# One table of order, slots and engines for another: linear attention and a three-way feed-forward layer on one core

## The chip, the cores and the metric

The kernel runs on one core of one Trainium2 chip. The metric is the device time of that core in microseconds, as the median of several runs. The core has five engines with queues of their own: TensorE (PE, matrix products), VectorE (DVE), ScalarE (ACT), GpSimd (POOL) and SyncE (SP, which here only issues DMAs). POOL and ACT issue DMAs as well.

## The reference

Inputs and output are float32. The kernel computes in bfloat16, with the sums of products in float32.

```python
# q, k, v: (8 batches, 8 heads, 576 tokens, 64); w_phi: (64, 128)
def phi(x):
    proj = x @ w_phi
    proj = proj - max(abs(proj), axis=-1)
    return concatenate([exp(proj), exp(-proj)], axis=-1)
q_p, k_p = phi(q), phi(k)
kv = k_p.T @ v;  z = sum(k_p over tokens)
attn = (q_p @ kv) / (q_p . z + 1e-6)
x = attn as (4608 tokens, 512)
h = max(max(x @ w1, x @ w2), x @ w3)        # d_ff = 768
out = h @ w_out
```

The attention has no softmax over the tokens, so that all of a head's keys go into one matrix kv before its queries use it.

## The kernel before

**Attention.** The work is cut into 16 units. Unit u holds four heads of batch u // 2. For each unit the kernel loads q and k by POOL's DMA queue, which turns them into bf16 on the way (qk_bf, L432 and L442); the 64 last tokens of each head, the "tail", and v come by SP (tail_raw L475, v_raw L484). Then q and k are turned. In units 0 to 3 TensorE does that (tps, L508); from unit 4 on it is a DMA transposition issued by SP (qkT<-qk_bf, L527; 128x10x128 for the keys with the tails, 128x8x128 for the queries). TensorE projects by w_phi (L545, products of 64 rows), VectorE takes the largest absolute values (mk and mq, L549), ScalarE the exponentials of the keys (Ek, L553) and of the queries (Eq, L633). The factor of the keys' largest value goes into the values: POOL multiplies v by em (vab, L597). Then come the key-value products (kvps, L616, 64 rows), a second projection (psm, L642 and L650), the numerators with the denominator beside them (psn, L683), their sums on VectorE (y, L692 and L695), the reciprocal (rden, L740), and the division on POOL (x_sb, L741). The quotient is turned again, from unit 2 on by a DMA transposition on SP (xT<-x_sb, L773).

**Feed-forward layer.** Nine chunks: one of 512 tokens for each batch, and a ninth of all the tails (8 x 64 tokens). The weights come by POOL's queue; the kernel holds w2 - w1 and w3 - w1 (L987), so that the maximum over three becomes a relu of one difference (L905, L907) and a maximum with the other (L901), while the part through w1 goes straight through w1 times w_out (pm, L1023). A chunk then has up products (ups, L891), the straight products (L924), the down products (ops, L929), the evictions (osb<-ops, L939, on ScalarE or VectorE, into one of four buffers) and the stores (L943, on SP's queue but for one). The seventh, eighth and ninth chunk are computed with seven up products in the place of eight (L820): this needs four sums of quarters of xT for each chunk (sums, L799, on VectorE or POOL), joins on VectorE (parts and hT, L829), relu on ScalarE (L862) and a maximum on VectorE (hx in the code, hT<-hT,parts at L864).

**Order.** Everything is recorded first as a list of 1688 steps, each with the steps that it depends on and the buffers that it uses. Nothing is scheduled when the kernel is built: PLAN, a table of words written out in the program, gives for each step its engine, the slots of its buffers and its place. A word such as

```python
19T0@4.8      # step 19, TensorE, slot 0, start at 4.8
```

names the step, the engine (T, D, A, G, S for PE, DVE, ACT, POOL, SP), the slots and a planned start. plan() reads it and returns the steps in the order in which they are issued; each engine then runs its own steps in that order and waits by semaphores for what it depends on. The planned start has one more use: fill() puts products on a constant tile (idler, L1071) into the planned gaps of TensorE in the first 30 us.

Of the kernel before, what the change touches and what calls it, by code (L numbers as in the profile page):

```python
# [90 lines left out]
1D@0.8 4A@1.1 103G0@1.2 10S0@0.7 3S@1.1 9G1@1.9 8G@2.6 2D@0.9 16S0@1.7 11A@3.9 12D@3.9 7D@4.1 5D@4.3 102G@3.4 0G@4.1 19T0@4.8 20D0@5.2  # L91
6A@4.2 29T12@5.7 31A0@6.2 30A0@6.6 35D0@6.2 186G2@4.6 17G@8.4 104G@8.6 259G3@8.8 260G@9.6 106T3@7.3 107D1@8.0 13S@3.1 112T45@8.7
34A@7.1 33A@7.6 119T67@8.9 32D@8.6 114A1@9.1 185G@10.3 187S1@3.5 118D1@9.2 121A@9.6 113A1@10.1 110T0@9.2 25T3@9.4 111D@9.8 125D@9.9
122D@10.6 26D@11.2 15D@11.5 117A@10.6 23T2@11.4 18S1@4.9 123A@11.1 116A@11.5 120A@12.0 24A@12.5 124A@13.0 1166G@11.0 188G@11.8
1169G@12.0 51T10@11.8 115D@11.7 52D0@12.3 27T3@12.1 28D@12.9 14D@13.1 73T56@12.6 53D@13.3 74A0@13.4 105S2@5.6 1167G@12.7 75A0@13.9
76A@14.4 77A@14.9 21T2@13.5 22D@13.9 43T74@13.8 48T13@13.9 46D@14.3 49D@14.6 47D@15.2 50D@15.5 54A0@15.3 68T05@14.6 36T62@15.5
126T14@15.7 70A@15.6 44A@16.0 45A@16.3 69A@16.6 71A@17.0 72A@17.5 129D@16.1 42D@16.5 41A@18.0 333G1@13.9 334S0@9.0 108T3@16.3
130D1@17.1 39D@17.4 109D@18.0 78T7@16.8 190T0@17.2 1168G@15.2 141A1@18.5 80A@18.7 191D2@18.6 134T54@18.8 55G0@16.0 56G@17.1 403G0@18.5
261G@19.2 57G@19.4 265T3@19.1 58A@18.9 40A@19.1 131T02@19.8 135D@19.2 136D@19.8 266D3@20.4 62T54@20.5 144G1@19.6 59G@19.7 61G@20.8
60G@20.9 128A@19.6 79A@19.9 37A@20.1 127A@20.6 38A@20.9 137A@21.4 64A0@21.6 133D@21.0 132D@21.6 63D@22.2 151T37@21.1 263T1@21.5  # L100
153A1@21.7 152A1@22.2 81A0@22.7 194T6@21.9 195D@22.4 264D@22.6 65T42@22.2 67D@23.2 66D@23.4 155A@22.9 154A@23.3 85T05@22.8 82T36@23.1
161T1@23.5 86D0@23.6 192T2@23.6 162A@23.8 163A@24.1 83D@24.0 87D@24.4 193A@24.4 84D@24.8 90T47@24.0 156T01@24.5 91D1@25.2 93T35@25.0
402G@22.0 140G@22.8 139G@22.9 138G@24.0 142G@25.1 157A@25.2 94D@25.6 145T26@25.4 164A1@25.7 92D@26.0 95D@26.4 1188T4@26.1 160A@25.9
146A1@26.4 147A@26.6 1192T3@26.5 1189D0@26.8 165T75@27.0 158A@26.7 168T26@27.3 88D0@27.4 166D2@27.5 169D@27.9 404G@26.2 143G@26.4
332G@27.5 89G0@28.2 335G@29.4 1193A@27.2 159A@28.1 167D@28.3 96D1@28.7 170D@28.8 171D2@29.4 148T40@27.7 97G@29.7 1190T7@28.4 150A@28.6
149A@28.7 301T23@28.9 1191A@29.0 173T15@29.2 176T60@29.6 172G1@30.9 337S0@35.1 189S3@36.5 174D0@29.8 177D@30.2 175D@30.6 98T4@29.9
1198T7@30.1 178D@31.0 99D@31.4 753S0@42.1 303A0@29.9 302A0@30.4 305A@30.9 304A@31.4 262S1@42.8 406S1@43.5 179D0@31.8 276T16@31.5
196T50@31.8 267T4@32.1 1200T2@32.2 612S1@47.0 277A0@32.0 280A@32.4 1199D@31.9 281A0@32.9 180G@32.1 202D0@32.5 268D@33.1 279D1@33.3
100T3@33.5 183T7@33.8 1170G@33.6 1172G@35.7 101D@34.0 184D@34.4 282D@34.8 199D@35.4 1196T4@34.0 181T3@35.3 200A1@33.4 201A1@33.9
1201A@34.4 278A@34.8 1197A@35.5 182D@36.0 203T76@35.7 215T02@35.9 291T14@36.2 206D@36.4 1194T3@36.5 208A@36.1 197A@36.6 198A@37.1  # L110
205A@37.6 1195A@38.1 293D0@37.0 217D1@37.6 292D@38.2 204A@38.5 1214T5@38.0 216D@38.8 269T34@38.9 283T21@39.2 287D@39.5 1171G@37.8
1212T7@39.4 210T01@40.3 1215A1@39.0 207A@39.5 284A@40.0 275D@39.8 1173G@39.9 1175G@42.0 285A@40.3 271A@40.5 214D@40.7 213D@41.0
1213D@41.3 1206T5@40.5 274A@41.0 212A@41.5 211A@41.8 1207A@42.0 270A@42.5 273A@43.0 1204T1@41.4 1210T7@42.3 1211A@43.5 286D@41.9
336S2@48.6 209D@42.2 221A0@43.9 1205D@42.8 272D@43.4 1208T0@43.1 306T54@44.1 1209D@44.2 218T72@44.3 308A@44.5 307A@45.0 228T61@44.5
219D@44.8 407S@49.3 220D@45.4 1226T3@44.9 288T05@45.8 1174G@44.1 1218T7@46.1 289D@46.2 1227D@46.9 1224T2@47.0 224G0@46.2 1219D@47.5
290D@48.0 1225D@48.6 222G@46.5 229A1@45.5 294A1@46.0 309A@46.1 231A@46.6 310A@47.1 241A0@47.6 232A1@47.8 230A@48.3 233T03@48.0
236A@48.7 237A@49.2 223G@48.5 1216T7@48.3 238T5@49.1 339T24@49.4 1217D@49.4 353T16@49.6 225T37@50.5 342D0@50.0 356D@50.6 357D1@50.9
# [985 lines left out]
```

## Time and profile before

| | |
|---|---|
| time, three runs | 280.34, 281.12, 281.60 us; median 281.12 |
| profiled execution | 280.52 us, of which the span is 278.7 |
| granted TensorE clock | 0.999 of full speed, mean |
| PE busy | 269.0 us, 97% of the span |
| weight load of PE (overlaps) | 161.7 us, 58% |
| DVE | 243.5 us, 87% |
| ACT | 212.9 us, 76% |
| POOL | 186.7 us, 67% |
| DMA | 44.54 MB, mean 160 GB/s |

The profile shows one execution. Its span runs from the first instruction to the last; 1.8 us of the measured time lie outside. A line of the profile names the line of the program, the engine and the tiles (output<-inputs). The chain of waits is followed back from the last instruction: at each step to what released it, or to the instruction before it on its engine. A group in the page gives the busy time, the mean length of one and the idle time of the engine just before, with what ended it.

### The profile page before, as it was taken

The page shows a single profiled execution, that of the slowest core. Times are in us where ns is not written, and L with a number is a line of the kernel's source. Part 1 is how long each engine was busy: PE and PEld are TensorE (multiplying, and loading weights), DVE is VectorE, ACT ScalarE, POOL GpSimd, SP SyncE. Part 2 cuts the span into 40 slices and gives each one's busy share as a digit, 9 for nine tenths or more (in the row PEclk, how much of TensorE's full clock was granted, in tenths as well). Part 3 has the DMA queues.
Part 4 walks back from the last instruction along what each step waited for, and adds up shares of the span by engine and source line. Part 5 has one row for each costly group of instructions (what it writes and reads, how often), then busy time and mean ns, then how long its engine had stood idle before and what let it go on. Part 6 is the DMA issues. An engine that isn't in the chain of part 4 may idle for free.

```text
span 278.7 us, 8796 instructions
## 1 busy us (share of the span) xinstructions
PE 269.0 (97%) x3561; PEld 161.7 (58%) x3561; DVE 243.5 (87%) x497; ACT 212.9 (76%) x507; POOL 186.7 (67%) x184
## 2 busy tenths in 40 slices
PE   7989999999999989999999999999999998999993
PEld 5657654566555645555655456555548765686651
DVE  3899999999999869879889998999889999999950
ACT  3899999998899979598977999698988523254241
POOL 6789999998679634896397795888798844500000
PEclk9999999999999999999999999999999999999999
DMA  7999999999999999989999994940421242003434
GB/s 125 262 232 209 209 196 309 221 200 255 178 215 231 195 200 189 175 224 206 201 188 196 276 132 121 187 137 2 123 46 43 78 94 78 0 1 115 109 71 161
DMA packets 76216, 44.54 MB, mean 160 GB/s; under 512 B 52688, under 2 KB 67344, under 8 KB 76176
## 3 DMA queue, kind: packets, MB, share of 16 engines
q1 hardware_dynamic: 61184, 32.19, 53.6%
q0 software_dynamic: 14912, 11.77, 28.7%
q8 instruction: 28, 0.46, 0.7%
q14 instruction: 12, 0.10, 0.1%
q10 hardware_dynamic: 80, 0.03, 0.0%
HBM read 34.64 MB, written 9.44 MB: 158 GB/s over the span
## 4 chain that ended last, share of the span: by engine, by line
PE 83%; DVE 6%; ACT 4%; DMA 3%; issue 2%; POOL 1%; DVEq 0%; ACTq 0%; POOLq 0%
PE ups L891 23%; PE ops L929 15%; PE ops L924 10%; PE ups L820 7%; PE psn L683 7%; PE kvps L616 6%; PE psk L545 3%; PE psm L642 3%; DMA qkT<-qk_bf 3%; PE psq L545 3%; PE pm L1023 2%; ACT Ek L553 2%; DVE parts L829 2%; PE tps L508 1%; DVE hT L864 1%
## 5 line engine op out<-in xcount | busy, mean ns | idle before, releaser
L633 ACT ACTIVATE Eq<-psm 128x512 bf16<-128x512 f32 (+1 forms) x160 | 80.3, 583 | 6.8 <-PE psm L642 4.8
L553 ACT ACTIVATE Ek<-psk 128x512 bf16<-128x512 f32 x128 | 72.5, 639 | 5.8 <-PE psk L545 5.3
L597 POOL TENSOR_TENSOR vab<-v_raw,em 128x1152 bf16<-128x1152 f32 (+1 forms) x36 | 68.2, 1908 | 10.9 <-ACT em L591 10.9
L891 PE MATMUL ups<-xT,w_bf 128*128 128x512 bf16 x288 | 70.1, 379 | 0.0
L741 POOL TENSOR_TENSOR x_sb<-y,rden 128x640 bf16<-128x640 f32 x32 | 39.9, 1256 | 25.2 <-DVE rden L740 20.3
L929 PE MATMUL ops<-wout_bf,hT 128*128 128x512 bf16 (+2 forms) x222 | 52.1, 373 | 0.8 <-DVE hT L864 0.8
L549 DVE TENSOR_REDUCE mq<-psq 128x4 f32<-128x512 f32 x64 | 40.9, 681 | 4.0 <-PE psq L545 3.6
L549 DVE TENSOR_REDUCE mk<-psk 128x4 f32<-128x512 f32 x64 | 42.3, 681 | 1.7 <-PE psk L545 1.5
L891 PEld LDWEIGHTS <-w_bf 128*128 128x128 bf16 x288 | 25.0, 98 | 26.8 <-issue 1.7
L692 DVE TENSOR_TENSOR y<-psn,sq 128x325 f32<-128x325 f32 x64 | 30.3, 489 | 7.0 <-PE psn L683 6.2
L929 PEld LDWEIGHTS <-hT 128*128 128x128 bf16 x222 | 20.5, 98 | 22.1 <-DVE hT L864 1.3
L683 PEld LDWEIGHTS <-Eq 128*128 128x128 bf16 x640 | 26.5, 98 | 11.2 <-issue 0.9
L939 ACT COPY osb<-ops 128x512 f32<-128x512 f32 x28 | 16.8, 599 | 20.5 <-PE ops L929 19.6
L695 DVE TENSOR_TENSOR y<-y,psn 128x325 f32<-128x325 f32 x64 | 29.6, 484 | 1.5
L829 DVE TENSOR_TENSOR parts<-ups,parts 128x512 f32<-128x512 f32 (+1 forms) x45 | 29.1, 679 | 0.5
L683 PE MATMUL psn<-kv_sb,Eq 128*128 128x65 bf16 x640 | 28.9, 194 | 0.1
L545 PEld LDWEIGHTS <-qkT 64*128 64x128 bf16 x576 | 18.2, 94 | 15.4 <-issue 10.8
L901 DVE TENSOR_TENSOR hT<-hT,ups 128x512 bf16<-128x512 bf16 x36 | 23.9, 681 | 1.4 <-PE ups L891 1.0
L862 ACT ACTIVATE hT<-hT 128x512 bf16<-128x512 bf16 x18 | 10.7, 625 | 18.5 <-DVE hT L829 18.5
L924 PE MATMUL ops<-xT 128*128 128x512 bf16 x96 | 24.7, 380 | 0.0
L616 PE MATMUL kvps<-vab,Ek 64*128 64x65 bf16 x1152 | 22.1, 191 | 0.6 <-issue 0.5
L616 PEld LDWEIGHTS <-Ek 64*128 64x128 bf16 x1152 | 20.1, 94 | 2.5 <-issue 0.6
(85 smaller groups left out, 395.3 us busy)
## 6 DMA issues: line engine op xcount, KB each, us to landing
v_raw<-in_v_dram SPq DMA_DIRECT2D x16, 576.0 KB, 5.4
out_dram<-osb SPq DMA_DIRECT2D x32, 256.0 KB, 2.8
qk_bf<-in_k_dram POOLq DMA_DIRECT2D x15, 288.0 KB, 8.5
qk_bf<-in_q_dram POOLq DMA_DIRECT2D x15, 256.0 KB, 7.6
w_bf<-in_moe_w_dram POOLq DMA_DIRECT2D x3, 768.0 KB, 19.5
tail_raw<-in_q_dram SPq DMA_DIRECT2D x16, 64.0 KB, 5.5
wout_bf<-in_moe_w_out_dram POOLq DMA_DIRECT2D x1, 768.0 KB, 16.6
out_dram<-osb SPq DMA_DIRECT2D x6, 128.0 KB, 2.4
```

Of the source, the lines that this page charges most:

```text
L545: nc.tensor.matmul(ps[s]()[:, i, :], lhsT=qkT()[r, n, :], rhs=wph[r, :], start=True, stop=True)
L549: return nd(kind, {"DVE": 0.598 if n == 4 else 0.331}, lambda: nc.vector.tensor_reduce(dst(m()), ps()[:, 0:n, :], AXX, ALU.max, apply_abso ...
L553: return nd("ek", {"ACT": 0.478 if n == 4 else 0.264}, lambda: nc.scalar.activation(dst(Ek[g]()), ps()[:, 0:n, :], EXP, scale=1.0 - 2.0 * ...
L597: made.append(chosen(n_, lambda n_, g=g, t0=t0, t1=t1: (nc.vector if n_.eng == "DVE" else nc.gpsimd).tensor_tensor(vab()[:, g, t0:t1, 0:D] ...
L616: nc.tensor.matmul(kvps[ab]()[:, pr, g, :], lhsT=Ek[g]()[r, t, :], rhs=vab()[r, g, t, :], start=(pr == prs[0] and g + j == 0), stop=(pr == ...
L633: return nd("eq", {"ACT": 0.478 if n == 4 else 0.264}, lambda: nc.scalar.activation(Eq[g]()[:, t0:t0 + n, :], ps()[:, 0:n, :], EXP, scale= ...
L683: nc.tensor.matmul(psn[g]()[:, i, :], lhsT=Eq[g]()[:, t, :], rhs=kv()[:, pr, ab, g, :], start=True, stop=True)
L741: divs[pr] = nd("x", {"POOL": 1.2}, lambda pr=pr, y=y, rden=rden: nc.gpsimd.tensor_tensor(x_sb()[:, pr].rearrange("p t a d -> p a t d"), y ...
L829: return ff("uj", {"DVE": 0.598}, lambda: nc.vector.tensor_tensor(runs(dst()) if dst not in own else dst(), runs(ps()), runs(src()), ALU.add),
L891: nc.tensor.matmul(ups()[:, o * n:(o + 1) * n], lhsT=w_bf[i + (not plain)][:, ct, jj * P:(jj + 1) * P], rhs=tokens_of(ct)[:, cols] if halv ...
L924: nc.tensor.matmul(ops_()[:, 0:hi - lo], lhsT=tile_of(ct, tt), rhs=line_w[c_i > MOVE][:, ct, lo:hi], start=(ct == 0), stop=False)
L929: nc.tensor.matmul(ops_()[:, 0:hi - lo], lhsT=hT()[:, j, tt * P:(tt + 1) * P], rhs=wout_bf[:, j, lo:hi], start=plain and j == 0, stop=(j = ...
```

## The change

Only PLAN is another. The steps, their products, the functions and the line numbers are those of before. The first line of the table, before and after:

```diff
 PLAN = """
-1D@0.8 4A@1.1 103G0@1.2 10S0@0.7 3S@1.1 9G1@1.9 8G@2.6 2D@0.9 16S0@1.7 11A@3.9 12D@3.9 7D@4.1 5D@4.3 102G@3.4 0G@4.1 19T0@4.8 20D0@5.2
...
+3A@0.7 1D@0.8 4A@1.3 6D@3.7 103G0@1.2 10S0@0.7 5D@3.9 11A1@4.0 7A@4.3 9G@1.9 8G@2.6 0G@3.4 2D@4.1 12D@4.2 19T0@4.6 20D0@5.1 29T12@5.6
...
 """
```

59 of the 1688 steps change their engine: 26 go from VectorE to ScalarE and 21 back, 4 from POOL to ScalarE and 3 back, 2 from VectorE to POOL and 2 back, and the load of w_phi goes from SP to ScalarE. TensorE has the same products in another order, and 51 of the fillers at L1071 where there were 63. The slots are dealt out anew throughout. Three places of the order follow, each before and after. The numbers in the names only tell tiles apart, and are dealt anew in each build.

The first place is SP's queue around the transposition of unit 8's keys (qkT<-qk_bf in ten blocks, 128x10x128). The two rows of x_sb are the quotients of units 4 and 5, in this order; the rows of eight blocks are queries, and L943 is a store. Before:

```order
L943 DMA out_0_dram<-osb_1903 128x512
L773 DMA_TRANSPOSE xT_75<-x_sb_2089 128x10x128
L943 DMA out_0_dram<-osb_1810 128x512
L527 DMA_TRANSPOSE qkT_2526<-qk_bf_2126 128x10x128
L773 DMA_TRANSPOSE xT_75<-x_sb_2335 128x10x128
L527 DMA_TRANSPOSE qkT_2592<-qk_bf_2124 128x8x128
```

After:

```order
L943 DMA out_0_dram<-osb_1901 128x512
L527 DMA_TRANSPOSE qkT_1930<-qk_bf_1504 128x8x128
L475 DMA tail_raw_2166<-in_q_dram 64x4x64 x2
L527 DMA_TRANSPOSE qkT_2206<-qk_bf_2050 128x10x128
L773 DMA_TRANSPOSE xT_75<-x_sb_2180 128x10x128
L484 DMA v_raw_2242<-in_v_dram 128x2x576
L475 DMA tail_raw_2351<-in_q_dram 64x4x64 x2
L773 DMA_TRANSPOSE xT_75<-x_sb_2280 128x10x128
```

The transposition of unit 8's keys stood behind the quotient of unit 4 and a store; now it stands ahead of that quotient, and the store is not between them.

The second place is VectorE at the last maxima of the seventh chunk (L864 on tiles of 2x256) and the first joins of the ninth (hT of 16x32). Before:

```order
L829 TENSOR_TENSOR parts_5219<-ups_5416,parts_5446 128x512
L829 TENSOR_TENSOR hT_5259<-ups_5455,parts_5446 128x2x256
L829 TENSOR_TENSOR hT_5259<-ups_5468,parts_5411 128x2x256
L829 TENSOR_TENSOR parts_5387<-ups_5402,parts_5411 128x512
L829 TENSOR_TENSOR hT_5532<-ups_5510,parts_5526 128x16x32
L799 TENSOR_TENSOR sums_5534<-xT_75 128x512
L864 TENSOR_TENSOR hT_5259<-hT_5259,parts_5387 128x2x256
L864 TENSOR_TENSOR hT_5259<-hT_5259,parts_5219 128x2x256
```

After:

```order
L829 TENSOR_TENSOR hT_5213<-ups_5436,parts_5415 128x2x256
L829 TENSOR_TENSOR hT_5213<-ups_5426,parts_5410 128x2x256
L829 TENSOR_TENSOR parts_5209<-ups_5386,parts_5415 128x512
L799 TENSOR_TENSOR sums_5468<-xT_75 128x512
L799 TENSOR_TENSOR sums_5468<-sums_5468,xT_75 128x512
L864 TENSOR_TENSOR hT_5213<-hT_5213,parts_5182 128x2x256
L864 TENSOR_TENSOR hT_5213<-hT_5213,parts_5209 128x2x256
L829 TENSOR_TENSOR hT_5523<-ups_5481,parts_5501 128x16x32
```

VectorE had one sum there, of the eighth chunk; now it has two, of the ninth chunk, ahead of the last pair of maxima. On POOL the same stretch is the end of its work. Before (sums_5491 are the ninth chunk's, sums_5534 the eighth's):

```order
L1056 COPY x_late_76<-xT_75 128x4x64
L799 TENSOR_TENSOR sums_5491<-xT_75 128x512
L799 TENSOR_TENSOR sums_5491<-sums_5491,xT_75 128x512
L799 TENSOR_TENSOR sums_5491<-xT_75 128x512
L799 TENSOR_TENSOR sums_5534<-sums_5534,xT_75 128x512
L799 TENSOR_TENSOR sums_5491<-xT_75,sums_5491 128x512
L799 TENSOR_TENSOR sums_5534<-xT_75 128x512
L799 TENSOR_TENSOR sums_5534<-xT_75,sums_5534 128x512
```

After (sums_5468 are the ninth chunk's, sums_5525 the eighth's):

```order
L1056 COPY x_late_76<-xT_75 128x4x64
L799 TENSOR_TENSOR sums_5468<-xT_75 128x512
L799 TENSOR_TENSOR sums_5468<-xT_75,sums_5468 128x512
L799 TENSOR_TENSOR sums_5525<-xT_75 128x512
L799 TENSOR_TENSOR sums_5525<-sums_5525,xT_75 128x512
L799 TENSOR_TENSOR sums_5525<-xT_75 128x512
L799 TENSOR_TENSOR sums_5525<-xT_75,sums_5525 128x512
```

The ninth chunk's second and third sums went from POOL to VectorE, and the eighth chunk's first from VectorE to POOL.

The third place is SP's queue from the keys of unit 4 to the values of unit 4. The three value loads before are those of units 2, 10 and 3, in this order. Before:

```order
L527 DMA_TRANSPOSE qkT_895<-qk_bf_408 128x10x128
L484 DMA v_raw_897<-in_v_dram 128x2x576
L484 DMA v_raw_918<-in_v_dram 128x2x576
L484 DMA v_raw_926<-in_v_dram 128x2x576
L527 DMA_TRANSPOSE qkT_928<-qk_bf_469 128x10x128
L475 DMA tail_raw_962<-in_q_dram 64x4x64 x2
L484 DMA v_raw_1135<-in_v_dram 128x2x576
L527 DMA_TRANSPOSE qkT_928<-qk_bf_469 128x8x128
```

After (the value loads are those of units 2, 3, 4 and 6):

```order
L527 DMA_TRANSPOSE qkT_624<-qk_bf_330 128x10x128
L484 DMA v_raw_836<-in_v_dram 128x2x576
L527 DMA_TRANSPOSE qkT_880<-qk_bf_575 128x10x128
L475 DMA tail_raw_948<-in_q_dram 64x4x64 x2
L484 DMA v_raw_1094<-in_v_dram 128x2x576
L484 DMA v_raw_1124<-in_v_dram 128x2x576
L484 DMA v_raw_1153<-in_v_dram 128x2x576
L527 DMA_TRANSPOSE qkT_624<-qk_bf_330 128x8x128
```

The values of unit 3 were issued right behind those of units 2 and 10, and now stand behind the keys of unit 5 and a tail load.

More of the change, by code (lines that the diff above doesn't have):

```diff
@@ L239 @@
[L239 removed]
+3A@0.7 1D@0.8 4A@1.3 6D@3.7 103G0@1.2 10S0@0.7 5D@3.9 11A1@4.0 7A@4.3 9G@1.9 8G@2.6 0G@3.4 2D@4.1 12D@4.2 19T0@4.6 20D0@5.1 29T12@5.6
+34A0@6.0 32D0@6.0 35D@6.7 106T3@7.4 102G@3.9 260G2@4.6 16S0@1.1 186G3@5.3 185G@6.1 259G@6.8 104G@8.1 31A@6.8 30A0@7.3 110T4@8.5
+111A1@8.8 33A@9.1 1166G@8.3 17G@9.1 107D@8.1 112T56@8.8 118D1@9.3 119T70@9.1 115D@9.9 13S@2.5 15D@10.5 25T1@10.0 1169G@10.0 14D@10.7
@@ new lines @@
+1404T6@193.0 1049A@193.9 1405A@194.1 1050A@194.6 1110T14@194.0 1117T07@194.2 1020D@193.9 1113D@194.4 1120D@195.0 1121D1@195.3
+1116D@195.7 957S@192.0 1416T5@194.4 1420T6@195.3 1021T32@196.1 1417D@196.3 1022D@196.9 1421D@197.3 1412T7@196.4 1418T5@197.3
+1061G0@192.4 1060G@194.5 1112A@195.2 1111A@195.7 1128A1@196.4 1118A@196.6 1119A@196.9 1115A@197.2 1114A@197.7 1145T3@198.2
+1010T61@198.3 1146A0@198.5 1023D@197.9 1419D@198.4 1011D@199.0 1024D1@199.4 1147A1@198.7 1413A@199.0 1131G1@196.8 1129G@196.9
@@ L240 @@
+1553D@263.7 1586T2@261.9 1587T@262.8 1588D0@264.3 1562D@264.9 1590T3@264.1 1583T@265.0 1589S@265.1 1674S@265.7 1584A1@266.5 1585S@267.1
+1543D@265.3 1595T@266.3 1596D2@267.8 1597S@268.5 1591T@267.6 1592A0@269.1 1593S@269.7
 """
```

288 lines of the change are left out of this document (140 added, 148 removed).

## The prediction

> **What bounds the kernel now.** I read the page first, then the busy time by stretch, the waits of TensorE, the chain of waits and single stretches of the timeline. On the page, the shares of the chain by engine:
>
> ```profile
> PE 83%; DVE 6%; ACT 4%; DMA 3%; issue 2%; POOL 1%; DVEq 0%; ACTq 0%; POOLq 0%
> ```
>
> TensorE carries 83% of the chain. A busy TensorE need not be at its peak, so I cut the span where its state changes (columns: stretch, length, then busy us of PE, PEld, DVE, ACT, POOL, granted clock, DMA share, GB/s):
>
> ```profile
> 0.00:27.00 27.00, 23.80 (x357) 16.83 (x359) 20.95 (x49) 21.84 (x56) 21.68 (x37) 1.00 1.11 207
> 27.00:92.00 65.00, 64.66 (x970) 37.61 (x970) 61.86 (x133) 62.23 (x150) 57.68 (x50) 1.00 1.19 223
> 92.00:101.00 9.00, 7.98 (x141) 4.46 (x140) 6.51 (x13) 7.31 (x21) 6.21 (x5) 1.00 1.28 189
> 101.00:211.00 110.00, 109.95 (x1588) 60.97 (x1587) 97.40 (x199) 94.76 (x231) 80.33 (x74) 1.00 0.88 162
> 211.00:232.50 21.50, 20.64 (x243) 14.67 (x236) 21.02 (x44) 9.89 (x23) 15.98 (x17) 1.00 0.22 56
> 232.50:267.00 34.50, 34.48 (x251) 23.88 (x250) 32.88 (x59) 13.77 (x25) 4.77 (x5) 1.00 0.20 63
> 274.60:278.70 4.10, 0.00 (x0) 0.00 (x0) 0.00 (x0) 0.59 (x1) 0.00 (x0) 0.94 0.17 65
> ```
>
> From 27 us on TensorE stops only in two places, for 1.0 us of 9.0 around 92 to 101 and for 0.9 us of 21.5 before 232.5, and the last 4.1 us are the last eviction and store. Before 27 us it is not the bound: part of its 23.8 us are the filler products of L1071. The waits of TensorE name both places (us in total, times, longest):
>
> ```profile
> PE psk L545 <- DMA qkT<-qk_bf: 1.0, 1, 1.0
> PE ops L929 <- DVE hT L864: 0.8, 1, 0.8
> ```
>
> The change leaves the products as they are, so it can win only in such waits, in what a product costs by its neighbours, and in the first 27 us.
>
> **1. Fewer changes between forms of product.** The chain shows what a change costs (start, us, what):
>
> ```profile
> 46.17 0.97 PE ups L891 x4
> 47.14 0.33 PE psq L545 x8
> ...
> 54.01 0.37 PE psn L683 x10
> 54.37 0.87 PE ups L891 x4
> ```
>
> Four up products take 0.97 us when the rows next to them are 64-row products (L545, L616, L642), and 0.87 when they follow full ones (L683): 0.10 us for a change. Counted over the whole printed order, leaving out the fillers and L650, which runs in either form, there are 114 such changes before and 102 now. From the first L924 on, where every TensorE microsecond counts, there are 73 before and 67 now. I take 6 x 0.10 = **-0.6 us**; the bounds are 0 and all 12, -1.2.
>
> **2. The keys of unit 8.** The wait of 1.0 us is for a transposition on SP's queue; SP's timeline, with the POOL operation that released the first of its rows, and the transposition in the chain:
>
> ```profile
> 90.02 1.84 SPq L773 DMA_TRANSPOSE xT<-x_sb  x1
> 91.91 0.57 SPq L943 DMA_DIRECT2D out_dram<-osb  x1
> 92.59 3.14 SPq L527 DMA_TRANSPOSE qkT<-qk_bf  x1
> ...
> 88.72 1.27 POOL L741 TENSOR_TENSOR x_sb<-y,rden 128x640 bf16<-128x640 f32 x1
> ...
> 92.59 7.32 DMA qkT<-qk_bf
> ```
>
> The transposition stands third. The first row waits for POOL's x_sb, which ends at 89.99; the second, a store, for its eviction; so the third is issued at 92.59, lands 7.3 us later, and the product on it starts at once. The new order puts it ahead of both. Two things then set its issue: SP's turn, and its own load, here (POOL's queue, start, us):
>
> ```profile
> 79.31 1.47 POOL L442 DMA_DIRECT2D qk_bf<-in_k_dram  x2
> ...
> qk_bf<-in_k_dram POOLq DMA_DIRECT2D x15, 288.0 KB, 8.5
> ```
>
> The second of the two loads, at 80.07, is unit 8's. With the median landing of 8.5 us it is there at 88.6, four microseconds before the old issue, and POOL now issues it ahead of that x_sb product. So the transposition should be out by 88.6 at the latest, and the wait of 1.0 is gone: **-1.0 us** (bounds 0 and -1.0; nothing else stands behind that wait). What is late next is the pair of the x_sb transposition and the store behind it; the x_sb one still follows its POOL product, and the eviction that next wants the store's buffer has three others to take first.
>
> **3. VectorE and POOL in the last part.** The wait on hT L864 begins in two maxima of VectorE that run beside POOL's sums (start, us):
>
> ```profile
> 226.61 0.75 DVE L864 TENSOR_TENSOR hT<-hT,parts 128x512 bf16<-128x512 bf16 x2
> 227.46 1.89 DVE L829 TENSOR_TENSOR parts<-ups,parts 128x512 f32<-128x512 f32 x3
> 229.26 2.27 DVE L864 TENSOR_TENSOR hT<-hT,parts 128x512 bf16<-128x512 bf16 x2
> ...
> 228.80 1.15 POOL L799 TENSOR_TENSOR sums<-xT 128x512 bf16<-128x512 bf16 x1
> 230.03 1.22 POOL L799 TENSOR_TENSOR sums<-sums,xT 128x512 bf16<-128x512 bf16 x1
> 231.21 1.33 POOL L799 TENSOR_TENSOR sums<-xT 128x512 bf16<-128x512 bf16 x1
> ...
> 211.29 0.41 DVE L799 TENSOR_TENSOR sums<-xT 128x512 bf16<-128x512 bf16 x1
> ```
>
> The same pair takes 0.75 us alone and 2.27 beside three POOL sums, each ending where a POOL sum ends: 1.5 us of VectorE, of which TensorE felt 0.8. In the new order POOL makes only the first of the ninth chunk's sums; VectorE itself makes the next two (0.41 each), just ahead of the last pair of maxima, and POOL's other sums wait for those two. One other sum goes from VectorE to POOL in each of two places (the seventh and the eighth chunk), so VectorE's total there stays. I take **-0.8 us** (bounds 0, if another pair collides, and -1.5). Against it: five POOL sums now run in a row, 5 x 1.2 = 6.0 us, and on VectorE the first maximum of the ninth chunk's hT stands only the pair and eight L829 behind, 0.75 + 8 x 0.6 = 5.5 us (the three L829 from 227.46 to 229.26 take 0.6 each). A collision costs one of them up to 2.27 - 0.75 = 1.5; I take **+0.3** (bounds 0 and 1.5).
>
> The Trainium skill, SBUF — State Buffer, section "SBUF: two separate sides", calls the port pair of VectorE and GpSimd an exclusive lock: whoever starts first keeps it for the whole instruction, and a VectorE operation with two SBUF inputs is among those that wait. The trace agrees: 2.27 against 0.75. By that rule the two sums moved to VectorE can be held like the maxima; held once each by a POOL sum they would cost up to 1.2 each, and the sum below would be 2.4 higher. They stand behind POOL's only earlier sum, so I don't count on it.
>
> **4. The first 57 us.** POOL sets the pace there. Its values for unit 1 and the product that waits for them, then the four values of units 2 and 3:
>
> ```profile
> 23.45 3.38 POOL L597 TENSOR_TENSOR vab<-v_raw,em 128x576 bf16<-128x576 f32 x3
> 26.91 0.36 PE L616 MATMUL kvps<-vab,Ek 64*128 64x65 bf16 x12 [0.46 <-issue]
> ...
> 47.11 4.21 POOL L597 TENSOR_TENSOR vab<-v_raw,em 128x1152 bf16<-128x1152 f32 x2
> 51.42 4.21 POOL L597 TENSOR_TENSOR vab<-v_raw,em 128x1152 bf16<-128x1152 f32 x2
> ...
> 56.61 1.38 PE kvps L616 x72
> ```
>
> TensorE's key-value product at 26.91 starts at the end of POOL's third operation (26.83), and that at 56.61 one microsecond after the last one (55.63). What TensorE gains before 56 us therefore counts only as far as POOL is earlier. POOL has the same values, the same six weight differences and as many loads between; two small copies of unit 1's and 2's sums go to ScalarE, and the first values stand earlier. I take the wait of 0.46 as gone and passed on: **-0.5 us** (bounds: 0, and -1.5, about half of the 3.2 us that TensorE idles before 27).
>
> **5. The values of unit 3.** Their load moves back on SP's queue, behind the keys' transposition of unit 5 and a tail load. Before:
>
> ```profile
> 36.78 2.12 SPq L484 DMA_DIRECT2D v_raw<-in_v_dram  x3
> 39.87 5.62 SPq L527 DMA_TRANSPOSE qkT<-qk_bf  x1
> 45.53 1.30 SPq L475 DMA_DIRECT2D tail_raw<-in_q_dram  x2
> 46.88 0.60 SPq L484 DMA_DIRECT2D v_raw<-in_v_dram  x1
> ...
> DMA to landing us min/median/max: 7.2/7.2/7.2
> ...
> DMA to landing us min/median/max: 9.4/9.9/10.3
> ```
>
> The two last rows are the load at 46.88, and the two at 37.9 and 38.4, of which the second was unit 3's: it landed at 48.8, and POOL needed it at 51.42. Now it is issued after the transposition, at 39.87 plus 2 to 5.6, plus 1.3 for the tail: 43.2 to 46.8. With 7.2 to landing it is there between 50.4 and 54.0. The 5.6 us were spent behind three value loads, of which one is left there, so I lean to the early end and take **+0.3** (bounds 0 and 3.1).
>
> All else I cost at nothing: stores change places on SP, covered by four osb buffers; evictions change between ScalarE and VectorE one for one. If that cover fails, an eviction is late by its own length, the 0.59 us of ScalarE in the last row by stretch.
>
> **The sum.** -0.6 - 1.0 - 0.8 + 0.3 - 0.5 + 0.3 = -2.3 us against the profiled execution's 280.52 (span 278.7 and 1.8 around it): 278.2. That execution lies 0.6 us under the median of the three runs, 281.12; I go a third of the way and predict **278.4**. About 0.5%, 1.4 us, is what a measurement of this kernel tells from no change, so faster means under 279.7 and slower over 282.5.
>
> **The rivals.** (a) *The waits move.* For it: the new order is as tight as the old, and a wait of 1.0 us came from a single late landing among 24 transpositions. Against it: the two places are mended by the order itself. If 2 and 3 win nothing, -0.6 - 0.5 + 0.6 = -0.5 is left: 280.0, within 0.5%.
>
> (b) *Unit 3's values land late*, and this is the side on which it is slower. If the transposition takes its 5.6 us again, the load leaves at 46.8; with 10.3 to landing it is there at 57.1, POOL's two operations end at 61.3 instead of 55.1 (55.63 less 0.5), and the product behind them and everything after moves by 6.2 us: 278.2 - 0.3 + 6.2 = 284.1. With 7.2 it is 54.0, 3.1 late: 281.0, no change. It decides from a landing at 55.5 on, where the loss passes 4.6 us and the time 282.5. For it: TensorE has nothing between its turns that could be done instead, since its order is fixed. Against it: the load before it on the queue that stood longest has gone elsewhere.
>
> (c) *A colder clock.* The new order has 51 fillers for 63 at the start. The granted clock is 1.00 up to 27 us. If it fell to half for the 2.2 us that twelve fillers made (11.3 us busy for 63), up to 2.2 us would be lost and the time 280.4.
>
> ```profile
> L1071 PE MATMUL idler<-idle 128*128 128x256 bf16 x63 | 11.3, 308 | 1.3 <-DVE wph_low L379 1.1
> ```
>
> The Trainium skill, TensorE: Matmul & The Clock Gate, section "Part 1: The HAM clock gate", has the clock drop to half after an idle window of about 3.4 us. By that rule (c) needs a hole of that length; no row of before shows one.
>
> **How the numbers follow.** Forecast 0.60; (a) 0.20; (b) 0.17, of which 0.08 without change and 0.09 slower; (c) 0.03. About a quarter of (a) still falls under 279.7, and some of the forecast's own spread beyond it. Faster 0.62, no change 0.28, slower 0.10 (the last hundredth for what I have not seen). The range: from all gains at their bounds without a loss, -1.2 - 1.0 - 1.5 - 1.5 = -5.2 (275.3), I go up to 276.0, since not all of them come together; above it takes in (a), (c) and the milder (b) with its 281.0, to 281.8.
>
> **What would show it.** 1: chain rows of 0.97 for L891 become fewer against those of 0.87. 2: no wait of L545 on the DMA at about 98 us, and unit 8's transposition issued before 89. 3: all L864 pairs at about 0.75 us, no wait of L929 on L864. 4: no gap in the L616 of unit 1. 5: POOL's values of unit 3 start right behind those of unit 2. The prediction is wrong if new waits of TensorE of over 1 us stand between 57 and 275 us, or if POOL idles before unit 3's values.

## The result, and the profile after

The changed kernel takes 278.81 us (median of 22 runs, 277.60 to 281.48) against 280.39 us before (22 runs, 279.46 to 282.15). The ratio is 0.995, with a 95% interval of 0.9927 to 0.9973: faster, by 1.6 us. A second comparison gave 278.57 against 280.14, ratio 0.9946 (0.9926 to 0.9965). The forecast was 278.4, with a range of 276.0 to 281.8; its sum took 2.3 us off, and the medians differ by 1.6.

The first trace of the changed kernel doesn't show this gain at all. Its execution took 280.98 us, with a span of 279.0, longer than the 278.7 of before. So the kernel was profiled a second time (the run new_again below, 278.50 us, span 276.5), and the two traces of one and the same kernel are read side by side. First the shares of the chain of waits of the first trace and of the second:

```profile
PE 83%; ACT 7%; DMA 4%; DVE 2%; issue 2%; POOL 1%; POOLq 0%
```

```profile
PE 80%; DMA 8%; ACT 6%; issue 2%; POOL 1%; DVE 0%; SPq 0%; POOLq 0%
```

TensorE still carries the chain, and both waits that the prediction named are gone from it: no wait of L545 on a transposition, and none of L929 on hT L864 of more than 0.4 us. The largest waits of TensorE behind its start, in the first trace and then in the second (us in total, times, longest):

```profile
PE pwT L1013 <- issue: 1.0, 1, 1.0
PE ups L891 <- DMA xT<-x_sb: 0.9, 1, 0.9
```

```profile
PE pwT L1013 <- issue: 0.7, 1, 0.7
PE tps L508 <- DMA qk_bf<-in_k_dram: 0.7, 1, 0.7
```

A new wait on a quotient (xT<-x_sb) stands in the first trace and not in the second. The busy time by stretch of the second trace, for the stretches of the prediction (length, busy us of PE, PEld, DVE, ACT, POOL, granted clock, DMA share, GB/s):

```profile
0.00:27.00 27.00, 22.67 (x351) 15.72 (x351) 20.43 (x45) 21.29 (x59) 21.81 (x36) 1.00 1.10 208
27.00:92.00 65.00, 63.62 (x946) 36.66 (x948) 61.29 (x130) 62.31 (x155) 55.45 (x45) 1.00 1.19 206
92.00:101.00 9.00, 9.00 (x175) 5.70 (x172) 7.21 (x15) 8.31 (x23) 3.90 (x4) 1.00 1.27 234
211.00:232.50 21.50, 21.50 (x208) 14.99 (x205) 21.34 (x46) 8.17 (x16) 14.06 (x15) 1.00 0.23 55
```

From 92 us on TensorE has no gap, where before it had 1.0 us at 92 to 101 and 0.9 before 232.5. Ahead of 92 us it stops more than before (63.62 of 65.0, 64.66 before).

**Where the two traces of the changed kernel part.** It is in the first ten microseconds. TensorE's timeline (start, us, what) of the first trace, then of the second, then of before:

```profile
4.97 1.06 PE L1071 MATMUL idler<-idle 128*128 128x256 bf16 x4
...
6.61 2.74 PE L1071 MATMUL idler<-idle 128*128 128x256 bf16 x12
9.14 1.06 PE L508 MATMUL tps<-ident,qk_bf 128*128 128x128 bf16 x8
```

```profile
4.65 0.60 PE L1071 MATMUL idler<-idle 128*128 128x256 bf16 x4
...
5.66 1.49 PE L1071 MATMUL idler<-idle 128*128 128x256 bf16 x12
7.84 0.62 PE L508 MATMUL tps<-ident,qk_bf 128*128 128x128 bf16 x8 [0.69 <-DMA qk_bf<-in_k_dram]
```

```profile
5.27 0.60 PE L1071 MATMUL idler<-idle 128*128 128x256 bf16 x4
...
6.28 1.27 PE L1071 MATMUL idler<-idle 128*128 128x256 bf16 x10
7.38 0.61 PE L508 MATMUL tps<-ident,qk_bf 128*128 128x128 bf16 x8
```

Twelve fillers take 2.74 us in the first trace and 1.49 in the second; eight transpositions take 1.06 and 0.62. TensorE works at half its speed until about 10.3 us in the first trace, and until about 4 us in the second; before, it was quick from about 5 us on. The column of the granted clock shows 1.00 in all three. By POOL's weight differences the delay has arrived at the engine that sets the pace there (before, the first and the second trace of the changed kernel):

```profile
34.47 12.53 POOL L987 TENSOR_TENSOR w_bf<-w_bf 128x1024 bf16<-128x1024 bf16 x6
```

```profile
36.74 12.52 POOL L987 TENSOR_TENSOR w_bf<-w_bf 128x1024 bf16<-128x1024 bf16 x6
```

```profile
34.93 12.51 POOL L987 TENSOR_TENSOR w_bf<-w_bf 128x1024 bf16<-128x1024 bf16 x6
```

**A ruler for two orders.** Times of two traces can't be set against each other directly, since the orders differ. I took every weight load of TensorE but the fillers' (3498 in each trace), gave each the mean distance to the next one that its line has in the trace of before, and so know how much of the work each trace has begun at a time, read linearly between two loads. The table gives, where before had begun the work of so many us, how much later (+) or earlier (-) another trace had begun the same amount. The ruler has an error of its own, since a load's weight is a mean: with weights by line and tile in the place of the line alone, the entries of new_again move by up to 0.5, but the steps from one column to the next by no more than 0.15 us. The kernels of the lower rows are explained with the experiments.

```
before at (us)          29     93    108    195    222    232    243    272
first trace          +2.85  +2.27  +1.89  +1.31  +1.01  +0.20  +0.79  +0.36
new_again            +1.04  +0.60  -0.60  -1.18  -1.47  -2.28  -1.69  -2.13
keys8_ahead          +2.33  +2.33  +1.48  +1.49  +1.49  +1.46  +1.46  +1.46
sums_on_dve          +0.02  +0.02  -0.61  -0.61  -0.61  -1.56  -0.45  -0.72
head28_slots         -0.01  +0.06  -1.15  -1.73  -1.87  -2.68  -2.09  -2.52
head64_slots         +0.25  +2.86  +1.66  +1.20  +0.90  -0.03  +0.28  -0.15
head122_slots        +0.51  +0.52  -0.56  -1.05  -1.36  -2.28  -1.97  -2.40
head220_slots         0.00   0.00  -0.54  -0.54  -0.54  -1.37  -0.78  -1.21
new_no_fillers       +1.27  +0.76  -0.44  -1.02  -0.91  -1.76  -1.17  -1.60
head28_fewer_fillers +0.17  +0.23  -0.98  -1.57  -1.70  -2.52  -1.93  -2.36
```

The two traces of the changed kernel differ by 1.8 us at 29 us and by 1.7 at 93. From 93 to 108 us the first wins 0.8 less, which is its wait of 0.9 on a quotient, and from there on both win the same (1.53 each). So the first is the second with a slow start and one late landing.

### The profile page after: what moved, and what is told of

Same layout as the page of the kernel before. It is cut to its first block, busy times and chain, and to the rows that moved or that the text cites. A ratio compares the mean times of both kernels' runs of the same rounds, so it can differ in the third digit from the quotient of the medians.

```text
span 279.0 us, 8741 instructions
## 1 busy us (share of the span) xinstructions
PE 266.7 (96%) x3509; PEld 162.1 (58%) x3549; DVE 242.6 (87%) x492; ACT 212.7 (76%) x513; POOL 186.6 (67%) x183
## 4 chain that ended last, share of the span: by engine, by line
PE 83%; ACT 7%; DMA 4%; DVE 2%; issue 2%; POOL 1%; POOLq 0%
PE ups L891 22%; PE ops L929 15%; PE ops L924 10%; PE ups L820 10%; PE psn L683 7%; PE kvps L616 6%; ACT Ek L553 3%; DMA xT<-x_sb 3%; PE psk L545 3%; PE psm L642 2%; PE psq L545 2%; ACT Eq L633 2%; PE pm L1023 2%; PE idler L1071 2%; DMA wphi_f<-in_w_phi_dram 1%
## 5 line engine op out<-in xcount | busy, mean ns | idle before, releaser
L633 ACT ACTIVATE Eq<-psm 128x512 bf16<-128x512 f32 (+1 forms) x160 | 81.4, 588 | 8.0 <-PE psm L642 6.8
L891 PE MATMUL ups<-xT,w_bf 128*128 128x512 bf16 x272 | 68.6, 379 | 1.9 <-DMA xT<-x_sb 0.9
L929 PE MATMUL ops<-wout_bf,hT 128*128 128x512 bf16 (+2 forms) x215 | 51.3, 373 | 0.4
L891 PEld LDWEIGHTS <-w_bf 128*128 128x128 bf16 x288 | 25.3, 97 | 27.6 <-issue 2.2
L939 ACT COPY osb<-ops 128x512 f32<-128x512 f32 (+2 forms) x33 | 19.4, 589 | 19.4 <-PE ops L929 15.3
L929 PEld LDWEIGHTS <-hT 128*128 128x128 bf16 x222 | 20.6, 98 | 20.9 <-DVE hT L864 0.9
L829 DVE TENSOR_TENSOR parts<-ups,parts 128x512 f32<-128x512 f32 (+1 forms) x45 | 29.4, 685 | 1.0 <-PE ups L820 0.5
L545 PEld LDWEIGHTS <-qkT 64*128 64x128 bf16 x576 | 18.8, 94 | 14.5 <-issue 11.3
L924 PE MATMUL ops<-xT 128*128 128x512 bf16 x82 | 23.7, 380 | 0.7
L616 PE MATMUL kvps<-vab,Ek 64*128 64x65 bf16 x1152 | 21.6, 191 | 0.6 <-DVE qkT L521 0.3
L616 PEld LDWEIGHTS <-Ek 64*128 64x128 bf16 x1152 | 20.0, 94 | 2.1 <-issue 0.5
```

What stands on the lines that cost most here:

```text
L545: nc.tensor.matmul(ps[s]()[:, i, :], lhsT=qkT()[r, n, :], rhs=wph[r, :], start=True, stop=True)
L616: nc.tensor.matmul(kvps[ab]()[:, pr, g, :], lhsT=Ek[g]()[r, t, :], rhs=vab()[r, g, t, :], start=(pr == prs[0] and g + j == 0), stop=(pr == ...
L633: return nd("eq", {"ACT": 0.478 if n == 4 else 0.264}, lambda: nc.scalar.activation(Eq[g]()[:, t0:t0 + n, :], ps()[:, 0:n, :], EXP, scale= ...
L891: nc.tensor.matmul(ups()[:, o * n:(o + 1) * n], lhsT=w_bf[i + (not plain)][:, ct, jj * P:(jj + 1) * P], rhs=tokens_of(ct)[:, cols] if halv ...
L924: nc.tensor.matmul(ops_()[:, 0:hi - lo], lhsT=tile_of(ct, tt), rhs=line_w[c_i > MOVE][:, ct, lo:hi], start=(ct == 0), stop=False)
L929: nc.tensor.matmul(ops_()[:, 0:hi - lo], lhsT=hT()[:, j, tt * P:(tt + 1) * P], rhs=wout_bf[:, j, lo:hi], start=plain and j == 0, stop=(j = ...
```

## The experiments

None of these kernels leaves out a part of the computation; the fillers of L1071 work on a constant tile and take no part in the result. Every ratio is against the runs of the kernel before on the same chip.

**1. The changed kernel again.** No edit.

> The changed kernel once more, to get a second trace and to have its time beside the mixed tables. In its first trace TensorE's fillers start 0.21 us apart until 10.3 us (0.11 in the trace of before from 5.3 us on), and POOL's weight differences begin at 36.74 us instead of 34.47. Theory A: this slow start is a matter of the single execution, not of the table; then executions differ by about 2.3 us, the median is about 278.8, and a trace with an early quick start has a span of about 276.5 with L987 of POOL at about 34.4. Theory B: the new head is slower in every execution; then L987 begins at about 36.7 again and the span is about 279.

Measured: 278.57 us (277.95 to 279.42), before 280.14, ratio 0.9946 (0.9926 to 0.9965); the trace has a span of 276.5 and L987 at 34.93. Theory A holds: the slow start belongs to the execution, not to the table. But the new head isn't free: with a quick start it is still about 1 us behind before at 29 us and 0.33 at 59. Its wait of 0.74 on L1013 accounts for 0.3 of that, since before has one of 0.46 on L616.

**2. Mixed tables, first attempt.** The words that before plans ahead of a cut, then the rest in the new order. Since the two tables have other steps behind them at a cut, the slots had to be dealt out again.

```diff
 PLAN = """
-(the new table's words)
+(before's words that are planned ahead of 28, 64 or 122 us, in before's order, slots dealt out again)
+(all other words, in the new table's order, slots dealt out again)
 """
```

> The table of before for all steps that it plans before 28 us, then the new order; slots dealt out again. Theory A (the head of the new table costs nothing by itself) and the forecast's term 4 (first 57 us, -0.5, of which about half lies here): 278.8 to 279.1. Theory B (the new head costs 2.3 us): about 276.5.

> The table of before up to 64 us, then the new order. By the forecast's terms 4 and 5 (-0.5 and +0.3 there), 0.2 us slower than the new table, about 279.0; the wait of unit 8's keys must be absent, as in the new table. If the gain lay in the first 64 us, the time is that of before, about 280.4.

> The table of before up to 122 us, then the new order. By the forecast, term 2 (unit 8's keys, -1.0) is lost again and terms 1 and 3 (about -1.0 together in the last part) stay: about 1.2 slower than the new table, 1.0 faster than before, 279.4. The wait on unit 8's keys must be back. Rival: the last part wins nothing, since each wait mended there comes back elsewhere; then it is as slow as before, 280.4.

Measured: 279.89 (ratio 0.9998, 0.9976 to 1.002), 284.51 (1.0158, 1.0138 to 1.0179) and 287.30 us (1.0266, 1.0244 to 1.0287). All three miss every expectation. The second, with before's own order up to 64 us, has waits of TensorE that before doesn't have (timeline, with the idle time and what ended it):

```profile
53.97 0.78 PE L642 MATMUL psm<-qkT,wph 64*128 64x512 bf16 x2 [0.93 <-ACT Eq L633]
...
60.30 1.02 PE L891 MATMUL ups<-xT,w_bf 128*128 128x512 bf16 x4 [0.77 <-DVE y L692]
...
65.35 1.02 PE L924 MATMUL ops<-xT 128*128 128x512 bf16 x4 [1.02 <-ACT kv_sb L623]
```

An up product doesn't use y, and a straight product doesn't use kv_sb: these are products that wait until the former tenant of their PSUM bank has been read. I had dealt out the slots by the program's order alone, also in the part where the order was before's.

**3. The same orders with other slots.** The slots of before are kept ahead of the cut; behind it each buffer takes the slot of the one that it follows in the new table, or of the one that is free longest by the table's times. Order and engines are those of the second attempt word by word; 462 of the 1688 words differ in their slots with the cut at 64 us, and 483 with that at 122.

```diff
-(slots by the order of release in the program)
+(slots of before ahead of the cut; behind it those that follow the same buffer as in the new table)
```

> The same order and the same engines as head64_before, word by word; only the buffer slots differ: those of before are kept up to 64 us, and behind it each buffer follows the one that it follows in the new table. In head64_before the slots were dealt out by another rule in the first 64 us, and TensorE waited 3 to 5 us between 27 and 92 us, mostly for PSUM banks that had not been read out (L924 on L623, L642 on L633, L891 on L692). If these waits come from the slots, this run has none of them, L987 begins at about 34.5, and the time is 278.8 to 279.2. If they come from joining two orders, it is 284.5 again.

> The same order and engines as head122_before, with the slots of before kept up to 122 us. If the 7 us of head122_before come from the slots: by the forecast term 2 (unit 8's keys) is lost and the last part's gain stays, 279.4; if the last part wins nothing by itself, 280.2, the time of before. If they come from joining the orders, 287.

Measured: 280.05 us (ratio 1.0003, 0.9977 to 1.0029) in the place of 284.51, and 278.23 (0.9944, 0.9924 to 0.9964) in the place of 287.30. So 4.5 and 9.1 us came from the slots alone. With the cut at 122 us the kernel is as fast as the changed one: the first 122 us of the new table win nothing that the median shows, and the forecast's 279.4 for this run was 1.2 too slow. With the cut at 64 us one wait of the joint is left (TensorE, then SP's queue):

```profile
76.80 0.59 PE L891 MATMUL ups<-xT,w_bf 128*128 128x512 bf16 x2 [2.17 <-DMA xT<-x_sb]
```

```profile
68.87 1.34 SPq L773 DMA_TRANSPOSE xT<-x_sb  x1
...
70.94 7.07 SPq L527 DMA_TRANSPOSE qkT<-qk_bf  x2
```

It is what this row of the table loses between 29 and 93 us (+0.56 at 72 us and +2.86 at 78), so this run says nothing on its question.

**4. Unit 8's keys alone.** One word of before's table moved.

```diff
+615S0@89.0          # unit 8's keys, L527
 401S@89.0           # quotient of unit 4, L773
 ...
 1235S@90.5          # store
 ...
-615S0@91.1
```

> The kernel before with one word of the table moved: unit 8's keys transposition (SP, L527) stands ahead of the quotient of unit 4 and the store, nothing else. By the forecast's term 2: the wait of 1.0 us on qkT<-qk_bf is gone, and the time falls by 1.0 to about 279.2. Rival (the waits move): the quotients of units 4 and 5 (xT<-x_sb) are now issued about 3 us later, TensorE waits for one of them instead, and the time stays at 280.2. In the first trace of the changed kernel TensorE waited 0.9 us for such a quotient, which speaks for the rival in part.

Measured: 280.85 us (279.88 to 281.98, 12 runs), before 280.18, ratio 1.0018 (0.9998 to 1.0038). In its trace the wait is gone, as forecast, and no other takes its place: from 93 to 108 us the table shows -0.85, and then nothing is given back. But the run isn't faster, and why is not settled. Its profiled execution had a slow start (+2.33 at 29 us, at 281.98 us the longest of the twelve). By their times half of its executions may have had one, since six lie at 279.88 to 280.55 and six at 281.16 to 281.98; but only one has a trace, before with the same head has 3 of 35 runs over 281, and the faster six lie no lower than its median of 280.18. One thing the traces do show: the wait of 1.0 us itself isn't there in every execution of before's order. In sums_on_dve, head220_slots and head122_slots SP issues this transposition in the same place as before, third behind a quotient and a store; the product behind it in the first two of them (start, us, what, and the wait):

```profile
99.33 0.40 PE L545 MATMUL psk<-wph,qkT 64*128 64x128 bf16 x8 [0.38 <-DMA qkT<-qk_bf]
```

```profile
99.42 0.40 PE L545 MATMUL psk<-wph,qkT 64*128 64x128 bf16 x8 [0.48 <-DMA qkT<-qk_bf]
```

In head122_slots there is none over 0.2. The four executions waited 1.02, 0.38, 0.48 and about 0 us, depending on when the transposition landed (7.32 us in the chain of before, 5.60 in that of sums_on_dve):

```profile
93.68 5.60 DMA qkT<-qk_bf
```

**5. The three sums alone.** Before's table, with the ninth chunk's second and third sum on VectorE and the eighth's first on POOL.

```diff
 1606G2@228.6
-1607G@229.7 1608G@230.7 ... 1521D3@232.3 ... 1522G@233.3 ... 1609G@234.4
+1608D@231.0 1607D@231.1 ... 1609G@232.3 1521G3@233.4 1522G@234.0
```

> The kernel before with the ninth chunk's second and third sum on VectorE in the place of POOL, and the eighth chunk's first sum on POOL in the place of VectorE, as in the new table; nothing else. By the forecast's term 3: the pair of maxima beside POOL's sums falls from 2.27 to about 0.75 us, TensorE's wait of 0.8 us on hT L864 is gone, and the time falls by 0.5 to 0.8, to about 279.5. Rival: the maxima meet another of POOL's sums (in both traces of the changed kernel such pairs still take 1.6 to 1.7), and the time stays at 280.2.

Measured: 280.33 us (ratio 1.0006, 0.9991 to 1.0021). The rival holds. VectorE, POOL and TensorE in its trace:

```profile
228.66 1.32 DVE L864 TENSOR_TENSOR hT<-hT,parts 128x512 bf16<-128x512 bf16 x2
...
234.75 2.27 DVE L864 TENSOR_TENSOR hT<-hT,parts 128x512 bf16<-128x512 bf16 x2
```

```profile
234.31 1.15 POOL L799 TENSOR_TENSOR sums<-xT,sums 128x512 bf16<-128x512 bf16 x1 [4.95 <-DVE sums L799]
235.41 1.33 POOL L799 TENSOR_TENSOR sums<-xT 128x512 bf16<-128x512 bf16 x1
```

```profile
236.80 0.60 PE L820 MATMUL ups<-sums,w_sums 128*128 128x256 bf16 x4 [0.95 <-POOL sums L799]
```

The pair that TensorE felt takes 1.32 in place of 2.27, and the wait of 0.8 on hT is gone: -0.95 between 222 and 232 us. Then POOL, which had waited 4.95 us for VectorE's sums, makes its own beside the next pair, which takes 2.27; and TensorE waits 0.95 for POOL's first sum of the eighth chunk (the row at 235.41), the very one that was moved there: +1.11 up to 243 us. The wait has moved from a product that needs a maximum to one that needs a sum.

**6. The cut at 28 and at 220 us, with proper slots, and no fillers.** The edits are those of 3, and for the last run one constant.

```diff
-WARM = 30.0
+WARM = 0.0
```

> The table of before up to 28 us, with the slots of before there, then the new order, each buffer behind the one that it follows in the new table. Set against the same amount of TensorE's work, the second trace of the changed kernel is 0.8 us behind that of before at 29 us and gains all that it gains later. Theory (the new head loses, the rest wins): the time is 0.8 under the changed kernel, 277.8, and beats both. Rival (the loss of the head is taken up later, since TensorE waits for POOL there anyway): as the changed kernel, 278.6.

> The table and slots of before up to 220 us, then the new order: only the last chunks are new, with the three sums moved as in sums_on_dve and everything around them. Set against TensorE's work, the traces of the changed kernel win about 0.5 to 0.7 us behind this point against before. Theory (the last part wins as a whole, though the three sums alone win nothing): 279.6. Rival (the gain of the last part is prepared by what stands ahead of 220 us): 280.2.

> The changed kernel without the 51 products of L1071 on a constant tile; they take no part in the result. Theory (the slow start is TensorE's clock, which the fillers bring up): transpositions and projections of the first 15 to 20 us take twice as long as in the second trace of the changed kernel, the quick start comes later than the 10.3 us of its first trace, and the time is 3 to 6 us above 278.6 (twelve us of work at half speed, partly beside idle time). If the fillers do nothing, 278.6 or a little less.

Measured: 278.77 us (278.21 to 278.84, ratio 0.9948, 0.9935 to 0.996); 279.30 (0.9987, 0.9958 to 1.0016); 279.71 (0.9987, 0.9972 to 1.0003). With before's head the trace is 1.05 earlier at 29 us than that of new_again, 0.54 at 93, and 0.4 are left of it at the end (-2.52 against -2.13). The median doesn't show it (278.77; the changed kernel 278.57 in its own comparison). The cut at 220 us keeps 0.67 behind 195 us (-0.54 to -1.21) by its trace; its interval doesn't tell that from nothing. Without fillers TensorE is slow until about 22 us (24 transpositions in 2.72 us, and later 16 in 1.14):

```profile
17.85 2.72 PE L508 MATMUL tps<-ident,qk_bf 128*128 128x128 bf16 x24
...
23.41 1.14 PE L508 MATMUL tps<-ident,qk_bf 128*128 128x128 bf16 x16
```

That costs 1.1 us of the median (279.71 against 278.57), not the 3 to 6 that I expected, and in its trace only 0.23 more at 29 us than new_again (this execution, 279.00 us, is among the three fastest of its ten). In these traces a TensorE that is slow for 22 us without fillers costs less than one that is slow for 10 us with them, 1.8 us. The rows of the two starts suggest why: in the slow one twelve fillers held TensorE until 9.14, and in the other the transpositions behind them started at 7.84, when their load had landed. The last run was to test this, and did not bear it out.

**7. Fewer fillers.** head28_slots with 46 fillers in place of 63.

```diff
-COLD = 5.0
+COLD = 12.0
```

> head28_slots with 46 fillers in place of 63: from 5 to 12 us the planner of the fillers counts 0.22 us for each (COLD is 12.0 for 5.0), as long as one takes while TensorE is slow. In executions that start quickly the spare fillers hide in idle time, so the median stays at 278.6 to 278.8. In those that start slowly the fillers stand in front of products that are ready: in the first trace of the changed kernel twelve of them hold TensorE until 9.14 us, where its second trace starts the same product at 7.84. Theory: the slow starts cost about 1 us in place of 2.2, and no run is more than 1.3 us above the median. Rival: with fewer products the quick start comes later in every execution, and the median rises towards the 279.7 of the kernel without fillers.

Measured: 279.08 us (277.78 to 281.42, 12 runs), ratio 0.9962 (0.9937 to 0.9986). The expectation fails: one run lies 2.3 us above the median, with a span of 279.2. Four runs lie at 277.8 to 278.4 and four at 279.6 to 279.7; whether the latter are slow starts at a lower price can't be said from times without traces. What is left is that fewer fillers bring nothing that can be measured.

No version beats the changed kernel clearly; head122_slots (0.9944) and head28_slots (0.9948) are as fast.

## Why the prediction was right, point by point

The number was right: 278.4 forecast, 278.81 and 278.57 measured. That it came so near is in part luck. The medians fell by 1.6 us where the sum said 2.3, and the forecast set out from 280.7 where before has 280.39 and 280.14. The spans fell by 2.2 between the two quick traces and by 1.9 between the medians of the second comparison (278.4 and 276.5). The rest went outside the span, a term that the prediction left at 1.8 us: it is 1.73 to 1.92 in the 86 runs of before whose spans are on record, and 1.95 to 3.64 in the 22 of the changed kernel, with a median of 2.16. The tables with before's order up to 220 us have 1.8 (head220_slots, sums_on_dve, keys8_ahead), and head122_slots has 2.05, so it seems to come with something between 122 and 220 us; its cause is open. Nor were the parts of the sum all right.

**1, changes of form: the price right, the gain not all theirs.** The traces have 114 changes before and 102 after. By the ruler, 8 of the 12 that are gone lie ahead of 93 us, where new_again wins nothing. The other 4 lie between 108 and 195 us, where it wins 0.58. The price of 0.10 was taken from two rows of the chain, but before's trace bears it out from 40 us on: to the start of what follows, four up products (L891) take 0.96 to 0.97 us ahead of a 64-row product (6 times) and 0.86 to 0.87 ahead of a full one (19 times); eight L545 take 0.31 on average ahead of a full one (15 times) and 0.22 to 0.23 ahead of another 64-row one (16 times). So four changes make 0.4 of the 0.58. Nor does the gain follow their number: head28_slots, with the same 4, wins 0.58 there, head122_slots with 2 fewer 0.49, and head220_slots with none 0.00. What the rest is, is open. Six were counted and four count; that -0.6 came out all the same is chance.

**2, unit 8's keys: the mechanism right, the price that of one execution.** The transposition is issued at 86.34 in new_again and the wait is gone, -1.20 in that stretch by the ruler. But 1.0 was what one landing cost. With 1.02, 0.38, 0.48 and 0 us in four executions the term is worth about 0.5 (their mean), and alone it didn't make the kernel faster. In the first trace of the changed kernel 0.9 came back as a wait on a quotient, as rival (a) has it; in new_again and keys8_ahead it didn't.

**3, VectorE and POOL: the wait went and a part came back.** Forecast -0.5 in sum; new_again wins 0.81 up to 232 us and loses 0.59 up to 243, -0.22. The step that failed is the size of the collision: two pairs of maxima still meet POOL's sums, in new_again:

```profile
227.92 1.65 DVE L864 TENSOR_TENSOR hT<-hT,parts 128x512 bf16<-128x512 bf16 x2
233.09 0.41 DVE L799 TENSOR_TENSOR sums<-xT 128x512 bf16<-128x512 bf16 x1
233.42 0.41 DVE L799 TENSOR_TENSOR sums<-sums,xT 128x512 bf16<-128x512 bf16 x1
233.76 1.70 DVE L864 TENSOR_TENSOR hT<-hT,parts 128x512 bf16<-128x512 bf16 x2
```

"All L864 pairs at about 0.75 us" was wrong. Before had two such pairs as well, that of 2.27 and a second one that the prediction passed over:

```profile
236.04 1.72 DVE L864 TENSOR_TENSOR hT<-hT,parts 128x512 bf16<-128x512 bf16 x2
```

Over 0.75 each, VectorE lost 2.5 us to them before and still loses 1.85. The 0.59 that came back is no single wait. Measured from one product's start to the next, against the median of the same line and shape, five products between 230 and 240 us of new_again are 0.06 to 0.19 late, 0.60 together: 0.42 behind VectorE's joins (L829) and 0.19 behind its second sum. That the joins are late because of the sums and the long pair ahead of them is argued, not shown. The two moved sums themselves weren't held: 0.41 each. The Trainium skill, SBUF — State Buffer, section "SBUF: two separate sides", has the engine that starts first keep the port pair for its whole instruction; the rows agree, in that only the maxima beside a sum of POOL are long, and the 2.4 us that this rule would have cost, had POOL's sums met VectorE's, did not come.

**4, the first 57 us: wrong.** I forecast -0.5; new_again is about 1 us late at 29 us and 0.33 at 59. The step that failed is the reading of the wait of 0.46: I took it for a wait for the third of POOL's operations, which ended at 26.83, right ahead of the product at 26.91. In head220_slots, with before's order there, POOL's third operation ends at 27.14, and the same product starts at 26.91 all the same (in keys8_ahead the operation ends at 28.74 and the product starts at 29.24):

```profile
23.77 3.37 POOL L597 TENSOR_TENSOR vab<-v_raw,em 128x576 bf16<-128x576 f32 x3
```

```profile
26.91 0.36 PE L616 MATMUL kvps<-vab,Ek 64*128 64x65 bf16 x12 [0.27 <-issue]
```

The wait belongs to a place in TensorE's stream. In all nine traces with 51 or 63 fillers it stands ahead of TensorE's 352nd product, the fillers counted, whatever product that is: the 25th of a group of L616 with before's head, and with the new one the fifth of a group of L1013:

```profile
26.54 0.40 PE L1013 MATMUL pwT<-ident,w_bf 128*128 128x128 bf16 x4
27.68 0.40 PE L1013 MATMUL pwT<-ident,w_bf 128*128 128x128 bf16 x4 [0.74 <-issue]
```

It lasts 0.27 to 1.00 us and ends 1.27 to 1.53 us after a packet of 16 KB has landed, on a DMA queue that the page lists as instruction (q8). In the five other traces the 352nd product starts 1.38 us or more behind that landing, and no wait over 0.1 us stands ahead of it. So TensorE most likely waits there for its own instructions; no experiment tests this. If so, no order of POOL's values removes it. The sign that I named, no gap in the L616 of unit 1, came true because the wait moved to another product, 0.28 longer.

**5, unit 3's values: nothing.** They are multiplied right behind the others (POOL, new_again), so the +0.3 and rival (b) fall:

```profile
47.41 6.26 POOL L597 TENSOR_TENSOR vab<-v_raw,em 128x1152 bf16<-128x1152 f32 x3
...
53.79 2.11 POOL L597 TENSOR_TENSOR vab<-v_raw,em 128x1152 bf16<-128x1152 f32 x1
```

**What I didn't name.** Between 195 and 222 us new_again wins 0.29, and from 243 to 272 us 0.44; all tables with the new order in the last part win the latter. No wait over 0.3 us and no change of form stands behind these. The 0.44 are small waits again: behind 243 us seven products of before are 0.05 to 0.19 late, 0.66 together, for joins of VectorE and ScalarE (L829, L845), and two of new_again, 0.12 together. Why the joins are in time there, and what the 0.29 is, stays open. Parts of the new table that I had not costed thus made up for the head, which is luck. In sum for new_again: +1.04 up to 29 us, -0.44 up to 93, -1.20, -0.58, -0.29, -0.81, +0.59, -0.44: -2.13.

**The rivals.** (a) is a good part of what happened in 3, and of the first trace in 2. (c), the colder clock, I gave 0.03 and tied to the smaller number of fillers. It happened, as a TensorE at half its speed with the granted clock at 1.00, but in both tables: the traces of the changed kernel and of keys8_ahead, which has before's head with its 63 fillers, were slow until 10.3 and 10.5 us; in the eleven other traces with fillers the quick start came between 3.8 and 6.7 us.

## What to carry to other kernels

A wait that ends with the landing of a DMA has the price of one execution in one profile; see it in several before it goes into a sum in full. A wait for which the profile gives no reason is not to be put down to the engine whose row happens to end beside it: count which instruction it stands ahead of, in several orders. Two orders of the same work are compared at equal work, not at equal time: the ruler of weight loads showed to about 0.15 us in which stretch each part of the gain lay, also in runs whose medians told nothing. An order alone is half a table: the same order with other buffer slots cost 4.5 to 9.1 us here.

## What the runs showed of the hardware

TensorE's speed at the start isn't settled by the table. With the same table it doubled at about 4 us in one execution and at 10.3 in another, worth 1.8 us, 0.6% of the time, and more than the change that was to be measured; the granted clock read 1.00 all the while. The Trainium skill, TensorE: Matmul & The Clock Gate, section "Part 1: The HAM clock gate", speaks of a free-running window of about 3.4 us, with a change around 4 us that moves by half a microsecond between runs. The quick starts here spread more widely, from 3.8 to 6.7 us, and the two late ones came 3.6 us and more behind the latest of them, which would be one window more. Why that window wasn't enough, though TensorE was busy in nearly all of it (from 3.5 to 6.9 us in the first trace), isn't settled by these runs. Nor had I expected that a slow start costs less without the fillers than with them (0.23 against 1.8 us at 29 us, beside a quick start with them); that they then hold up work that is ready is argued from two traces, not shown.
